# A matmul scheduler that knows the array's shape, scores in larger groups, and a full-height matmul for the count of grid steps

## The chip, the cores and the metric

The kernel runs on one core of a Trainium2 chip. The metric is the time of one execution on the device in microseconds (us). The engines are named as in the profile: PE is TensorE (matmuls; PEld is its weight load), DVE is VectorE, ACT is ScalarE, POOL is GpSimd, SP is SyncE, which issues most transfers.

## The reference, cut to what matters

Three layers follow each other. Attention over 4 batches and 8 heads of 576 positions: half of the heads see the last 32 positions (local), half see every 32nd (strided). Then a gated layer, and a layer of eight experts, to which the tokens are given greedily, the best score first, 288 tokens to each expert.

```python
def reference(q, k, v, w_a, w_b, w_out, w_gate, w1, w2):      # shortened
    scores = q @ k.T / sqrt(64); scores = where(mask, scores, -1e9)
    x = softmax(scores) @ v                    # 2304 tokens x 512
    x = ((x @ w_a) * (x @ w_b)) @ w_out        # 512 -> 1536 -> 512
    logits = (x @ w_gate).flatten()
    for idx in argsort(-logits):               # token, expert; capacity 2304 // 8
        ...                                    # the first free place that fits
    for e in range(8):
        out[assigned == e] = relu(x[assigned == e] @ w1[e]) @ w2[e]
    return out
```

## The kernel before

Every large product is made of three matmuls of a rounded type (f32r): high by high, high by low, low by high part of the operands. So each operand is split into a high part (ACT or POOL) and a low part (DVE) before PE reads it. By the names of PE's results, in order of time:

- `S`: scores of two heads at once, 64 rows by 64 columns of the array for each head, in chunks of 64 positions (local, 96 keys) or 54 (strided). `local_pair` makes nine chunks in groups of three, and `soft` then takes a group chunk by chunk: mask, minimum (DVE), exponential (ACT).
- `PT`, `O`: `P` transposed, and the product with `v` (96 or 54 rows by 64 columns). `out_split` makes `xh` (ACT) and `xl` (DVE) of it, the operands of the next layer.
- `ab`: the gated layer, 48 weight chunks `f`, each with `wh` and `wl`; 24 matmuls of 512 columns or a few more for each. The weights come as 64-bit words; ACT and DVE convert the first twelve chunks (`from_f64`, tiles `r`, `cc`, `w_f`) while PE works on attention and on the first chunks. `tp` and `pw` are the transposes and products of `gate_weights`, `pl` the logits.
- `px`: the second product of the gated layer, 18 times 36 matmuls. Between them stand the steps of `assign`: a search over a grid in seven phases of five steps. A step makes `I` (DVE), counts with 18 small matmuls `pc`, compares (`fe`, DVE), and `pd` carries the count of steps to all 128 rows. In four of five steps `pd` has 64 rows (`step64`, `fe[:T]`), in the last 65 (`step1`).
- `tpi`, `ph`, `po`, `tpo`: the experts. Rows are gathered (`xg`), transposed (`tpi`, one for each of four `kc`), split into `xeh` and `xel`, multiplied (`ph`, result `hh` and `hl`), multiplied again (`po`, copied to `oT`), transposed back (`tpo`, copied to `orow`) and scattered. Weight chunks are split into `w12h` (ACT or POOL) and `w12l` (DVE).

Nothing of this is issued where it is written. `Plan.add` records each operation with a priority (`plan.prio`, a time that `weave` deals out to the bulk of matmuls and to the chains beside it) and with what it depends on. `Plan.flush` then goes through a model of the engines' clocks: at each step it takes the engine that is free first, and of the operations that are ready there the one with the lowest priority number, and calls it. Each engine's queue is in this order on the chip. During the start (`fill`) the plan also puts in dummy matmuls `warm`, so that PE's clock stays up. A matmul's price (`price`) knows its size and type; what stood on PE before it has no influence on it.

Of the kernel before, what the change touches and what calls it, by code (L numbers as in the profile page):

```python
# [8 lines left out]
F32 = mybir.dt.float32  # L9
# [18 lines left out]
T = 64  # L28
STEPS = 5
BIG = 1.0e30  # L30

# [19 lines left out]
class Plan:  # L51
# [12 lines left out]
    def __init__(self, tc):  # L64
        nc = tc.nc
        self.tensor, self.vector, self.scalar, self.gpsimd, self.sync = (
            Engine(self, n, getattr(nc, n)) for n in ("tensor", "vector", "scalar", "gpsimd", "sync"))
        self.prio = 0.0
        self.floor = 0.0
        self.filler = None  # L70
        self.behind = None
        self.ops = []
        self.access = {}
        self.clock = {}
        self.free = {}
        self.live = set()
        self.held = set()
        self.turn = {}
        self.columns = {}
        self.lanes = [0.0] * 8  # L80
# [67 lines left out]
    def add(self, name, engine, method, args, kwargs):  # L148
# [19 lines left out]
        if name == "tensor":  # L168
            wide = method == "matmul" and mybir.dt.size(aps[1].dtype) == 4
            op.load = max(31.0, self.size(aps[1]) * (2 if wide else 1) / 2.4)  # L170
        op.users, op.tiles, op.reads, op.waits, op.ready, op.end = [], {}, set(), 0, self.floor, None
# [55 lines left out]
    def flush(self):  # L227
# [30 lines left out]
        for _ in range(len(self.ops)):  # L258
            while True:
# [18 lines left out]
                while later[e] and later[e][0][0] <= t:  # L278
                    op = heapq.heappop(later[e])[2]
                    heapq.heappush(now[e], (op.prio, op.index, op))  # L280
                op = heapq.heappop(now[e])[2]
                key, t0 = short(op)
                if key is not None:
# [13 lines left out]
            if e == "tensor":  # L297
# [3 lines left out]
                stretch = 1 if warm else 2  # L301
                t = max(t, clock.get("pass", 0.0) + op.load * stretch)
                clock["pass"] = t
                clock[e] = t + op.cost * stretch
# [36 lines left out]
def tile_attention_moe_moe(  # L341
# [192 lines left out]
    def soft(Sp, n, w, masks, P, nm, sm, place):  # L534
        t = apool.tile([128, 288], F32, name="t", bufs=3)[:, :n * w].rearrange("p (c k) -> p c k", c=n)
        for c, i in zip(range(n), place):
# [53 lines left out]
    def local_pair(n0):  # L590
# [4 lines left out]
        sm = apool.tile([128, 11], F32, name="sm", bufs=3)  # L595
        for c0, n in ((0, 3), (3, 3), (6, 3)):
            Sp = ps_acc("S") if b else ps_mm("S")
            for c in range(n):
                for h in range(2):
# [3 lines left out]
                                     start=True, stop=True)  # L603
            if c0 == 6:
                load_next(n0)
# [256 lines left out]
    def later(ns, g):  # L862
        yield 0, ns
        yield from g
# [11 lines left out]
    def begun(r):  # L876
# [8 lines left out]
                 later(8000, attention(0, (3,)))])  # L885
    split_w(0)
    weave(gated(0), [attention(1, (0, 2)), later(4000, attention(1, (1, 3)))], 0, 2000)
    weave(gated(1), [])
# [18 lines left out]
    nc.gpsimd.iota(grid, pattern=[[1, 96], [0, 2]], base=0, channel_multiplier=0, allow_small_or_imprecise_dtypes=True)  # L907
    step64 = acon.tile([T, 128], BF)
    nc.gpsimd.memset(step64, float(T))
    nc.gpsimd.memset(step64[0:1], 0.0)  # L910
    step1 = acon.tile([T + 1, 128], BF)
    nc.gpsimd.memset(step1, 1.0)
    nc.gpsimd.memset(step1[T:T + 1], 1.0 / 16)
    shifts = acon.tile([128, STEPS - 1, NC], I32)
    for s in range(STEPS - 1):
        nc.gpsimd.memset(shifts[:, s], 6 * (STEPS - 2 - s))
    fe = acon.tile([T + 1, 9], BF)
    nc.gpsimd.iota(fe[T:T + 1], pattern=[[1, 9]], base=0, channel_multiplier=0, allow_small_or_imprecise_dtypes=True)
# [57 lines left out]
    def assign():  # L976
# [76 lines left out]
        for ph in range(E - 1):  # L1053
# [3 lines left out]
            for step in range(STEPS):  # L1057
# [20 lines left out]
                if step + 1 < STEPS:  # L1078
                    nc.tensor.matmul(pd[:, 8:9], step64, fe[:T, 8:9], start=True, stop=True)
                    w = spool.tile([128, NC], BF, name="w")  # L1080
# [436 lines left out]
```

## Time and profile before

| | |
|---|---|
| median of 3 runs | 865.04 us (863.64 to 866.58) |
| the profiled execution | 861.87 us, of which the span of the core is 860.2 |
| PE busy | 839.2 us (98%), 6391 matmuls |
| PEld busy | 700.3 us (81%) |
| DVE busy | 501.2 us (58%) |
| ACT busy | 314.4 us (37%) |
| POOL busy | 167.8 us (20%) |
| share of PE in the chain that ended last | 91% |

A product of type f32 (`S`, `O`, `pl`, `pw`) leaves two records in the trace for each matmul of the program. Matmuls overlap in the pipeline: a busy time of 0.39 us for an `ab` says little, since the next one starts 0.23 us after it. Distances from start to start are what PE's timeline is read by. In a timeline, equal instructions that follow each other are one row with a count.

### The profile page before, as it was taken

What the parts mean: (1) busy time and instruction counts of PE and PEld (TensorE: products, weight loads), DVE (VectorE), ACT (ScalarE), POOL (GpSimd) and SP (SyncE); (2) the same over time, 40 slices, a digit from 0 to 9 for tenths busy, and PEclk for the clock granted to TensorE, in tenths of its full rate; (3) what the DMA queues carried; (4) which work ended last, traced back from release to release, by engine and by line L of the source; (5) the groups of instructions that cost most, each with busy time, mean ns of one, the idle gap of its engine ahead of it and who ended that gap; (6) DMA issues with size and microseconds to landing.
All of it is one profiled execution on the core that took longest, in us unless ns stands there. A gap on an engine that the chain in (4) does not pass through costs nothing.

```text
span 860.2 us, 16558 instructions
## 1 busy us (share of the span) xinstructions
PE 839.2 (98%) x6391; PEld 700.3 (81%) x6391; DVE 501.2 (58%) x1450; ACT 314.4 (37%) x840; POOL 167.8 (20%) x220
## 2 busy tenths in 40 slices
PE   8899999999999999999999999999999999999996
PEld 5677888777677777888777777778799999999995
DVE  5999984776464432222377777766166556655540
ACT  6978412465354311111333232222243333333330
POOL 2111321111111120111000000000145435653311
PEclk9999999999999999999999999999989999999998
DMA  9977963656342221121132212100156456655510
GB/s 316 372 278 240 319 222 121 210 176 205 121 154 83 74 74 50 50 74 50 64 121 72 77 50 74 51 24 27 52 188 210 140 179 203 229 173 173 176 30 27
DMA packets 34639, 118.90 MB, mean 138 GB/s; under 512 B 4768, under 2 KB 4768, under 8 KB 34560
## 3 DMA queue, kind: packets, MB, share of 16 engines
q1 hardware_dynamic: 31488, 108.43, 36.7%
q0 software_dynamic: 3072, 9.41, 3.5%
q8 instruction: 50, 0.82, 0.4%
q14 instruction: 29, 0.24, 0.1%
HBM read 98.98 MB, written 18.87 MB: 137 GB/s over the span
## 4 chain that ended last, share of the span: by engine, by line
PE 91%; DVE 3%; DMA 2%; ACT 2%; issue 1%; POOL 0%; POOLq 0%; DVEq 0%; SPq 0%; ACTq 0%
PE ab L158 34%; PE px L158 18%; PE po L158 12%; PE ph L158 12%; PE S L158 3%; PE pc L158 3%; PE pl L158 2%; PE O L158 2%; PE PT L158 2%; DMA r<-in_w_out_dram 1%; PE tpo L158 1%; PE tpi L158 1%; DVE cc L158 1%; PE pw L158 1%; ACT Ps L158 1%
## 5 line engine op out<-in xcount | busy, mean ns | idle before, releaser
L158 PE MATMUL ab<-xh,wh 128*128 128x512 f32 (+1 forms) x488 | 188.0, 386 | 0.6 <-ACT xh L158 0.6
L158 PE MATMUL ab<-xl,wh 128*128 128x512 f32 (+1 forms) x488 | 179.8, 369 | 0.0
L158 PE MATMUL ab<-xh,wl 128*128 128x512 f32 (+1 forms) x488 | 179.1, 367 | 0.0
L158 DVE TENSOR_TENSOR w12l<-w,w12h 128x1024 fp32r<-128x1024 f32 x64 | 78.1, 1222 | 54.3 <-PE po L158 22.3
L158 PEld LDWEIGHTS ab<-xh,wh 128*128 128x128 f32 x488 | 92.2, 189 | 20.0 <-issue 3.1
L158 PEld LDWEIGHTS ab<-xh,wl 128*128 128x128 f32 x488 | 92.3, 189 | 15.3
L158 POOL TENSOR_SCALAR wh<-wab 128x1024 fp32r<-128x1024 f32 x42 | 50.0, 1191 | 274.0 <-PE ab L158 220.4
L158 PEld LDWEIGHTS ab<-xl,wh 128*128 128x128 f32 x488 | 92.5, 190 | 12.5 <-issue 0.4
L158 DVE TENSOR_TENSOR G<-a_sb,ab 128x256 f32<-128x256 f32 x108 | 41.0, 415 | 96.0 <-PE ab L158 89.6
L158 PE MATMUL px<-wol,gh 128*128 128x512 f32 x216 | 87.1, 404 | 0.0
L158 PE MATMUL px<-woh,gh 128*128 128x512 f32 x216 | 86.9, 403 | 0.0
L158 ACT ACTIVATE a_sb<-ab 128x512 f32<-128x512 f32 (+1 forms) x61 | 33.3, 546 | 130.6 <-PE ab L158 116.8
L158 ACT ACTIVATE gh<-G 128x512 fp32r<-128x512 f32 x54 | 34.1, 632 | 124.5 <-PE px L158 119.1
L158 PE MATMUL ph<-xeh,w12h 128*128 128x288 f32 x256 | 78.3, 307 | 0.2 <-ACT xeh L158 0.2
L158 PE MATMUL po<-hh,w12h 128*128 128x288 f32 x256 | 77.7, 304 | 0.0
L158 PE MATMUL ph<-xeh,w12l 128*128 128x288 f32 x256 | 76.4, 299 | 0.0
L158 PE MATMUL ph<-xel,w12h 128*128 128x288 f32 x256 | 76.0, 297 | 0.2 <-DVE xel L158 0.2
L158 PE MATMUL po<-hh,w12l 128*128 128x288 f32 x256 | 75.6, 295 | 0.0
L158 PE MATMUL po<-hl,w12h 128*128 128x288 f32 x256 | 75.4, 295 | 0.0
L158 ACT ACTIVATE w12h<-w 128x1024 fp32r<-128x1024 f32 x36 | 38.1, 1060 | 53.4 <-PE po L158 36.2
L158 DVE TENSOR_TENSOR wl<-wab,wh 128x1024 fp32r<-128x1024 f32 x42 | 51.3, 1222 | 8.0 <-POOL wh L158 7.0
L158 POOL TENSOR_SCALAR w12h<-w 128x1024 fp32r<-128x1024 f32 x28 | 37.5, 1341 | 89.2 <-PE po L158 44.0
(367 smaller groups left out, 1565.7 us busy)
## 6 DMA issues: line engine op xcount, KB each, us to landing
w<-in_w_dram SPq DMA_DIRECT2D x64, 512.0 KB, 3.8
wab<-wab_dram SPq DMA_DIRECT2D x42, 512.0 KB, 3.7
r<-in_w_ab_dram SPq DMA_DIRECT2D x24, 512.0 KB, 7.2
qkT<-in_qk_dram SPq DMA_DIRECT2D x16, 608.0 KB, 5.8
r<-in_w_out_dram SPq DMA_DIRECT2D x12, 512.0 KB, 3.5
wab_dram<-w_f SPq DMA_DIRECT2D x12, 512.0 KB, 4.9
x_dram<-xr SPq DMA_DIRECT2D x17, 256.0 KB, 2.0
wo_dram<-w_f SPq DMA_DIRECT2D x6, 512.0 KB, 4.4
```

Source lines behind the costliest of these rows:

```text
L158: op.call = lambda: getattr(engine, method)(*args, **kwargs)
```

## The change

Three edits.

1. The plan's model of PE gets a shape: method, more than 64 rows, more than 64 columns, and whether the operand is f32r. A matmul of another shape than the one before costs 90 ns more in the model. When the operation that is first by priority has another shape than the last one issued, and a ready one has the last one's shape and a priority number less than 4000 above, that one is taken first.
2. The scores of the local heads come in two groups of five and four chunks instead of three of three; the tile `t` grows for it.
3. `step64`, `step1` and `fe` get 128 rows, the added ones zero, and every `pd` reads all 128.

```diff
+SLACK = 4000.0
+        self.slack = 0.0
+        self.shape = None
...
+            rows, cols = aps[1].ap[0][1], self.size(aps[1])
+            op.shape = method, rows > 64, cols > 64, aps[2].dtype == F32R
...
                 op = heapq.heappop(now[e])[2]
+                if e == "tensor" and self.slack and op.shape != self.shape:
+
+                    same = [x for x in now[e] if x[2].shape == self.shape and x[0] < op.prio + self.slack]
+                    if same:
+                        x = min(same)
+                        now[e].remove(x)
+                        now[e].append((op.prio, op.index, op))
+                        heapq.heapify(now[e])
+                        op = x[2]
...
                 t = max(t, clock.get("pass", 0.0) + op.load * stretch)
+                if op.shape != self.shape:
+                    t += 90.0
+                    self.shape = op.shape
...
-        t = apool.tile([128, 288], F32, name="t", bufs=3)[:, :n * w].rearrange("p (c k) -> p c k", c=n)
+        t = apool.tile([128, 480], F32, name="t", bufs=3)[:, :n * w].rearrange("p (c k) -> p c k", c=n)
...
-        for c0, n in ((0, 3), (3, 3), (6, 3)):
+        for c0, n in ((0, 5), (5, 4)):
...
+    plan.slack = SLACK
...
-    step64 = acon.tile([T, 128], BF)
+    step64 = acon.tile([128, 128], BF)
     nc.gpsimd.memset(step64, float(T))
     nc.gpsimd.memset(step64[0:1], 0.0)
-    step1 = acon.tile([T + 1, 128], BF)
+    nc.gpsimd.memset(step64[T:], 0.0)
+    step1 = acon.tile([128, 128], BF)
     nc.gpsimd.memset(step1, 1.0)
+    nc.gpsimd.memset(step1[T:], 0.0)
...
-    fe = acon.tile([T + 1, 9], BF)
+    fe = acon.tile([128, 9], BF)
+    nc.gpsimd.memset(fe, 0.0)
...
-                    nc.tensor.matmul(pd[:, 8:9], step64, fe[:T, 8:9], start=True, stop=True)
+                    nc.tensor.matmul(pd[:, 8:9], step64, fe[:, 8:9], start=True, stop=True)
```

`plan.slack` is set before the first `flush`, so it holds for every operation.

The order of the queues moves with it. First PE under the gated layer, at the scores of the second batch: `S` of 96 columns is a local head, of 54 a strided one. Before:

```order
L158 MATMUL S<-qkT 64x54 x10
L158 MATMUL ab<-xh,wh 128x512
L158 MATMUL ab<-xl,wh 128x512
L158 MATMUL ab<-xh,wl 128x512
L158 MATMUL S<-qkT 64x96 x6
L158 MATMUL ab<-xh,wh 128x512
L158 MATMUL ab<-xl,wh 128x512
L158 MATMUL ab<-xh,wl 128x512
L158 MATMUL S<-qkT 64x96 x6
```

and after:

```order
L161 MATMUL ab<-xh,wh 128x512
L161 MATMUL ab<-xl,wh 128x512
L161 MATMUL ab<-xh,wl 128x512
L161 MATMUL S<-qkT 64x96 x8
L161 MATMUL S<-qkT 64x54 x10
L161 MATMUL ab<-xh,wh 128x512
L161 MATMUL ab<-xl,wh 128x512
L161 MATMUL ab<-xh,wl 128x512
```

Two groups of scores that came at different places stand together, and fewer places in the row of `ab` are broken.

Then PE at the second `pd` of the assignment. Before:

```order
L158 MATMUL pc<-Cb,I 64x8
L158 MATMUL px<-wol_4747,gh 128x512
L158 MATMUL px<-woh_4746,gl__4768 128x512
L158 LDWEIGHTS step_3770
L158 MATMUL pd<-fe,step_3770 128x1
L158 MATMUL px<-woh_4746,gh 128x512
L158 MATMUL px<-wol_4747,gh 128x512
L158 MATMUL px<-woh_4746,gl__4768 128x512
L158 MATMUL px<-woh_4749,gh 128x512
L158 MATMUL px<-wol_4750,gh 128x512
L158 MATMUL px<-woh_4749,gl__4768 128x512
L158 LDWEIGHTS I
```

and after:

```order
L161 MATMUL pc<-Cb,I 64x8
L161 MATMUL px<-woh_4712,gl__4732 128x512
L161 MATMUL px<-woh_4726,gh 128x512
L161 LDWEIGHTS step_3747
L161 MATMUL pd<-fe,step_3747 128x1
L161 MATMUL px<-wol_4727,gh 128x512
L161 MATMUL px<-woh_4726,gl__4748 128x512
L161 MATMUL px<-woh_4726,gh 128x512
L161 MATMUL px<-wol_4727,gh 128x512
L161 MATMUL px<-woh_4726,gl__4748 128x512
L161 LDWEIGHTS I
```

The step keeps its place; five `px` instead of six stand between `pd` and the next `pc` here, and in later phases seven.

Last DVE at a border between two experts (the third of seven): each `xel` is one `kc` of the next expert's rows, and the last of them is `kc` 3. Before:

```order
L158 TENSOR_TENSOR w12l<-w_7375,w12h 128x1024
L158 TENSOR_TENSOR xel<-tpi,xeh 128x288
L158 TENSOR_TENSOR w12l<-w_7386,w12h 128x1024
L158 TENSOR_TENSOR xel<-tpi,xeh 128x288
L158 TENSOR_TENSOR w12l<-w_7397,w12h 128x1024
L158 TENSOR_TENSOR xel<-tpi,xeh 128x288
L158 TENSOR_TENSOR w12l<-w_7410,w12h 128x1024
L158 TENSOR_TENSOR xel<-tpi,xeh 128x288
L158 TENSOR_TENSOR w12l<-w_7404,w12h 128x1024
L158 TENSOR_TENSOR w12l<-w_7414,w12h 128x1024
```

and after:

```order
L161 TENSOR_TENSOR xel<-tpi,xeh 128x288
L161 TENSOR_TENSOR w12l<-w_7426,w12h 128x1024
L161 TENSOR_TENSOR w12l<-w_7437,w12h 128x1024
L161 TENSOR_TENSOR w12l<-w_7448,w12h 128x1024
L161 TENSOR_TENSOR xel<-tpi,xeh 128x288 x2
L161 TENSOR_TENSOR w12l<-w_7461,w12h 128x1024
L161 TENSOR_TENSOR w12l<-w_7455,w12h 128x1024
L161 TENSOR_TENSOR w12l<-w_7465,w12h 128x1024
L161 COPY orow<-tpo 96x512
L161 TENSOR_TENSOR xel<-tpi,xeh 128x288
```

The `xel` of `kc` 3 moves behind two more splits of weights and behind the copy of a `tpo`; on PE its `tpi` moves behind the first 18 `ph` of the new expert.

## Rows read from the trace of the kernel before

**Rows 1.** PE's timeline at a 64-row pd: start, length, instruction, idle before

```profile
548.90 0.39 PE L158 MATMUL px<-woh,gl__5026 128*128 128x512 f32 x1
549.22 0.17 PE L158 MATMUL pd<-fe,step 64*128 64x1 bf16 x1
549.33 0.50 PE L158 MATMUL px<-woh,gh 128*128 128x512 f32 x1
549.66 0.39 PE L158 MATMUL px<-wol,gh 128*128 128x512 f32 x1
```

**Rows 2.** PE's timeline at a 65-row pd

```profile
537.87 0.40 PE L158 MATMUL px<-woh,gh 128*128 128x512 f32 x1
538.11 0.18 PE L158 MATMUL pd<-fe,step 65*128 65x9 bf16 x1
538.15 0.47 PE L158 MATMUL px<-wol,gh 128*128 128x512 f32 x1
538.46 0.39 PE L158 MATMUL px<-woh,gl__4995 128*128 128x512 f32 x1
```

**Rows 3.** PE's timeline at two S visits among ab

```profile
65.05 0.79 PE L158 MATMUL S<-qkT 64*64 64x54 f32 x20
65.77 0.50 PE L158 MATMUL ab<-xh,wh 128*128 128x512 f32 x1
...
66.34 0.39 PE L158 MATMUL ab<-xh,wl 128*128 128x512 f32 x1
66.66 0.71 PE L158 MATMUL S<-qkT 64*64 64x96 f32 x12
67.30 0.50 PE L158 MATMUL ab<-xh,wh 128*128 128x512 f32 x1
67.64 0.39 PE L158 MATMUL ab<-xl,wh 128*128 128x512 f32 x1
```

**Rows 4.** PE's timeline, two groups of S together (20 and 12 records)

```profile
10.64 1.30 PE L158 MATMUL S<-qkT 64*64 64x54 f32 x32
11.87 0.39 PE L874 MATMUL warm<-ones_f 128*128 128x256 bf16 x2
```

**Rows 5.** PE's timeline at a visit of transposes among po

```profile
681.89 0.41 PE L158 MATMUL tpi<-ident,xg 96*128 96x96 f32 x3
682.08 0.38 PE L158 MATMUL po<-hh,w12h 128*128 128x288 f32 x1
682.30 0.29 PE L158 MATMUL po<-hl,w12h 128*128 128x288 f32 x1
```

**Rows 6.** Busy time in a window: us, PE, PEld, DVE, ACT, POOL, clock, DMA, GB/s

```profile
50.00:100.00 50.00, 50.00 (x427) 37.95 (x428) 48.95 (x149) 35.38 (x113) 9.66 (x13) 1.00 0.79 272
```

**Rows 7.** Timelines of DVE and PE at the twelfth weight chunk

```profile
118.12 1.21 DVE L158 TENSOR_TENSOR wl<-wab,wh 128x1024 fp32r<-128x1024 f32 x1
...
120.39 0.39 PE L158 MATMUL ab<-xh,wl 128*128 128x512 f32 x1
```

**Rows 8.** Timelines of ACT and PE around 217 us

```profile
216.43 0.67 ACT L158 ACTIVATE r<-r 128x512 int32<-128x512 uint32 x1 [2.11 <-DMA r<-in_w_out_dram]
...
217.58 0.61 PE L158 MATMUL pw<-lsel,wT 128*128 128x8 f32 x4 [1.80 <-ACT wT L158]
```

**Rows 9.** Busy time in the window behind it

```profile
220.00:222.00 2.00, 2.00 (x5) 1.61 (x6) 0.73 (x7) 1.19 (x6) 0.00 (x0) 0.50 0.77 203
```

**Rows 10.** Busy time in a window with eight tp in a row

```profile
160.00:163.00 3.00, 3.00 (x34) 2.22 (x33) 2.53 (x5) 1.75 (x4) 1.31 (x1) 1.00 0.51 175
```

**Rows 11.** Timelines of DVE and PE at a border between two experts

```profile
683.67 0.45 DVE L158 TENSOR_TENSOR xel<-tpi,xeh 128x288 fp32r<-128x288 f32 x1
684.04 1.22 DVE L158 TENSOR_TENSOR w12l<-w,w12h 128x1024 fp32r<-128x1024 f32 x1
687.94 0.68 DVE L158 COPY orow<-tpo 96x512 f32<-96x512 f32 x1
...
683.75 0.30 PE L158 MATMUL ph<-xeh,w12h 128*128 128x288 f32 x1
```

More of the change, by code (lines that the diff above doesn't have):

```diff
@@ L603, in local_pair @@
                                      start=True, stop=True)
-            if c0 == 6:
+            if c0 == 5:
                 load_next(n0)
```

## The prediction, made before the changed kernel was run

> **What bounds the kernel now.** I read the page's busy times first: TensorE (PE) is the engine that hardly rests. The windows by stage say the same of the middle: from 50 to 100 us PE is busy for all 50 us, and VectorE (DVE) for 48.95 of them [rows 6]. So until some 115 us there are two engines at their limit, and afterwards one. Up to about 42 us the start-up is paced by DVE and ScalarE (ACT), and PE fills the time with dummy matmuls; what the change does to PE there is worth nothing. From there to the end a nanosecond that PE saves is a nanosecond of the span, unless another engine is late next.
>
> A busy PE is not a PE at its peak, so the second view is PE's timeline, read by the distance from one start to the next. A px matmul starts 0.23 us after the one before it. Around a pd matmul of 64 rows the starts lie 0.32 (px to pd), 0.11 (pd to px) and 0.33 us (px to px) apart [rows 1]; around the last pd of a phase, which has 65 rows, they lie 0.24, 0.04 and 0.31 us apart [rows 2]. The second group is the key to the case. 65 rows already take the full height of the array, the shape of the px around it. So of 0.76 us the change of shape costs 0.17: 0.08 to 0.10 on the way in, 0.065 on the way out, 0.02 on the next weight load. Unrounded starts, averaged over the visits, give 766 against 592 ns: **174 ns for one pd**. The 0.31 us after the full-height pd is a weight load that a short matmul can't hide; it is there in both.
>
> The S visits show the same among the ab matmuls: 66.34 to 66.66 is 0.32 us (0.10 too long), the last S to the ab behind it, and then 0.34 instead of 0.23 us to the second ab (0.11 too long) [rows 3]. What the way out of S costs is seen where two groups of S stand together: 20 records alone hold PE from 65.05 to 65.77, 12 alone from 66.66 to 67.30 [rows 3], together 1.36 us; one after the other they hold it from 10.64 to 11.87, 1.23 us [rows 4]. So one exit is 0.13 to 0.14 us. **An S or O visit costs 0.10 + 0.14 for the two shape changes and 0.11 for the weight load of the ab behind it.**
>
> Transposes have ab's full shape. Three tpi between po matmuls stretch the two starts 681.89 to 682.08 and 682.08 to 682.30 [rows 5]; po alone runs at 0.13, so a visit of three costs some 0.28 us, 0.09 each, and has no price of its own. The new scheduler treats a transpose as another shape and charges 90 ns for it; the chip does not, so gathering transposes earns nothing.
>
> **The change part by part.** *The pd of 128 rows.* 28 of the 35 pd are of the 64-row kind: 28 x 0.174 = **-4.9 us**, with px on both sides in all 28. px here are not waiting for anybody, so all of it counts if DVE keeps pace: in between DVE makes the operand of the next pc, under six px before. In the first phase only five stand there now, 0.17 + 0.23 us less cover for each of some five steps; I take 0.3 us for that into the last term. The extra memsets on GpSimd stand far ahead of the first pd, behind other work, and cost nothing; if they were late, the first pc would wait once.
>
> *The preference for the shape that stands, and S in groups of five and four.* From the order of the two programs I count, between the last dummy matmul and the first logits, 69 visits to another shape before and 48 after, and 50 direct returns from one of them to an ab before, 25 after. 21 x 0.24 = 5.0 and 25 x 0.108 = 2.7: **-7.7 us**. Under the logits there is one visit less and five returns less: **-0.6 us**.
>
> *What DVE takes back.* 15 of the 42 shape changes and 9 of the 25 returns that go lie before 92 us, worth 2.8 us. There DVE converts and splits the weights, and its margin shrinks chunk by chunk: the twelfth wl ends at 119.33 (118.12 + 1.21), and the first ab that reads it starts at 120.39 [rows 7]. PE can come 1.06 us earlier and no more unless DVE does. DVE's work up to that place is the same in both orders. So between 0 (DVE's few idle moments close) and 1.7 us are given back: **+1.5**, near the upper end since DVE idles for 1 us in 50 [rows 6]. Behind that chunk the conversions are done and the margin grows again.
>
> *A stall that loses its place.* At 216 us ACT stands behind the landing of a w_out transfer, the copy of wT behind it, and PE waits 1.80 us for wT [rows 8]; its granted clock then falls to half, 0.50 from 220 to 222 us [rows 9], about 1 us more. Before, 4 ab stand between the two pw groups there; after, 15 (3.4 us). If the transfer lands as late, PE has work: between 0 and -2.8, I take **-2.0**.
>
> *What the reordering adds at the borders of the experts.* Before, the last tpi of the next expert (kc = 3) stands 12 po ahead of the first ph. After, it stands behind 18 ph, followed by four tpo, and ten ph later its xel is read. In DVE's queue that xel now stands behind three w12l and an orow copy. Count from the first ph, 683.75 in the trace of before, where a w12l starts 0.3 us later, at 684.04, because it needs a buffer that the last po frees [rows 11]. PE reaches the reader after 18 x 0.132 + 0.3 (tpi) + 0.43 (tpo) + 10 x 0.132 = 4.4 us. DVE: if one w12l is done by 1.0, two more end at 3.45, orow (0.68) at 4.15, xel (0.45) at 4.6 [rows 11], 4.75 with the hand-over: PE waits 0.35 us. If none is done before 0.3, xel ends at 5.1 and PE waits 0.85; and if a weight chunk lands late, 1.4. If DVE is ahead, 0. Seven borders: between 0 and 9.8, I take **+2.5**, by the buffer that [rows 11] shows.
>
> *Other new waits.* The plan now knows a shape change, so it brings PE to its operands closer to when they are there; before, PE came later than planned by 0.35 us a visit, and that was a cushion. O behind its PT copy, the first steps of the assignment, eight po ahead of the third tpi at the first expert, and S of five chunks at the start (0.3 us later to DVE): between 0 and 4, I take **+1.5**.
>
> Sum: -4.9 - 7.7 - 0.6 + 1.5 - 2.0 + 2.5 + 1.5 = **-9.7 us**. The profiled execution took 861.87 us (span 860.2), which is 0.37% under the median of the runs, 865.04. 852.2 / 861.87 = 0.989, on the median 855.3.
>
> A rule speaks against the grouping of transposes. The Trainium skill, TensorE: Matmul & The Clock Gate, section Part 4: PE-mode transpose, holds that transposes don't count as work for the clock gate. By that rule the longer runs, up to 15 where tpi, tp and PT now meet, would let the clock fall. In this trace a window with eight tp in a row has a granted clock of 1.00 [rows 10]; no run here shows 15.
>
> **The rivals.** *The conversions on DVE hold PE (chance 0.15).* All 2.8 us of the first part are given back, and the start loses its 0.3 us more: about 1.6 worse, 857. For it: DVE's 48.95 of 50 [rows 6]. Against it: the part after 120 us holds two thirds of the gain.
>
> *Slower: the late kc = 3 (0.07; 0.06 for its smaller form).* The place is DVE's queue at the seven borders. To end 0.3% above before, it has to eat 9.7 + 2.6 + 2.5 = 14.8 us, 2.1 a border: that is so from the point where the first of the three w12l starts 1.6 us after the first ph. It needs the weight transfers to be late every time. At 1.4 us a border the whole stands at about 862.6, within 0.3%. Against it: the w12l at 684.04 began without an idle moment of DVE before it [rows 11], so its weights were there.
>
> *Half clock behind long transposes (0.05).* Four runs of 9 to 15 transposes stand under ab; each fall would cost what the one after 216 us did, about 1.7 us: +6.8 in all, 858.9 on the profiled time and 862.1 on the median. It is the mechanism of the rule of the Trainium skill named above; the trace so far speaks against it [rows 10].
>
> *The pd doesn't change (0.05).* If it were the rows that hold data and not the rows addressed that count, the 4.9 us stay: 860.2. Against it: the 65-row pd holds data in 65 rows and goes at the full-height price.
>
> **How the numbers follow.** Forecast 0.62, 855.3 with its own range 851 to 859. The range that is to hold 8 in 10 takes in the bounds: nothing given back and the stall gone is -16, 849 on the median; upward the two rivals at 857 and 860 and half of the one at 862: 849.5 to 862. About 0.3%, 862.4 to 867.6, is what a measurement of this kernel can't tell from no change. Faster: 0.62 + 0.15 + 0.05 + 0.03 = 0.85. Same: 0.08. Slower: 0.07.
>
> **What would show it.** After the change px to pd should be 0.24 us and pd to px 0.04 at all 35 places, and every step of the assignment 0.17 us of PE shorter. S groups of 54 and 96 should stand together with one entry and one exit. At about 120 us the wl should end when PE asks for it, with a wait of up to 1.7 us. The wait of 1.80 us for wT should be gone, and the clock whole around it. At the borders of the experts the even row of ph should show one hole of some 0.35 us ahead of the ph that reads the xel of kc = 3. I am wrong if the pd keep 0.32 and 0.11, if the holes at the borders are 2 us, or if the first ab after the start-up comes more than 1 us later.

## The result, and the profile after the change

The changed kernel takes 854.9 us (median of four runs, 851.71 to 856.31), the kernel before 864.52 (863.64 to 866.58): a ratio of **0.988, 95% interval 0.9843 to 0.9917**. A later group of runs gave 854.55 against 860.66, 0.9915 (0.9886 to 0.9945). The ratios are the recorded ones; they lie up to 0.0017 from the quotients of the medians. The forecast was 855.3. The number fits; the way to it, as the traces show below, was another one in most of its steps.

The page after: the profiled execution took 856.28 us, above its median (before: 861.87, under its median), so the two traces stand only 5.6 us apart.

```profile
span 854.6 us, 16531 instructions
PE 824.9 (97%) x6384; PEld 697.5 (82%) x6384; DVE 501.0 (59%) x1450; ACT 311.3 (36%) x840; POOL 164.3 (19%) x223
```

PE's timeline at a pd that had 64 rows, to be held against [rows 1]:

```profile
548.55 0.39 PE L161 MATMUL px<-wol,gh 128*128 128x512 f32 x1
548.78 0.18 PE L161 MATMUL pd<-fe,step 128*128 128x1 bf16 x1
548.82 0.48 PE L161 MATMUL px<-woh,gl__5017 128*128 128x512 f32 x1
549.13 0.40 PE L161 MATMUL px<-woh,gh 128*128 128x512 f32 x1
```

The starts lie 0.23, 0.04 and 0.31 us apart, where they lay 0.32, 0.11 and 0.33 apart.

The window of [rows 6] (us, PE, PEld, DVE, ACT, POOL, clock): DVE is as busy as before, and PE, 50.00 before, idles for 3 us and loses clock.

```profile
50.00:100.00 50.00, 47.05 (x413) 36.91 (x412) 48.98 (x136) 31.22 (x102) 8.10 (x12) 0.97 0.77 251
```

What PE waits for between 45 and 445 us (engine, what waits, what for: us in total, times, longest), before and after:

```profile
PE pw L158 <- ACT wT L158: 1.8, 1, 1.8
PE pw L158 <- ACT woT L158: 0.6, 1, 0.6
```

```profile
PE O L161 <- ACT PT L161: 2.7, 2, 1.4
PE PT L161 <- DVE Ps L161: 1.1, 1, 1.1
PE pw L161 <- ACT woT L161: 0.9, 1, 0.9
PE S L161 <- PE O L161: 0.9, 1, 0.9
PE pl L161 <- ACT L L161: 0.9, 1, 0.9
PE ab L161 <- DVE wl L161: 0.7, 2, 0.6
PE O L161 <- DVE nm L161: 0.6, 1, 0.6
PE ab L161 <- ACT a_sb L161: 0.5, 1, 0.5
PE px L161 <- ACT gh L161: 0.3, 1, 0.3
```

That is 8.6 us of waits in place of 2.4. In the same window PE waits 2.4 to 3.6 us in the five traces whose attention has no preference (before, pd alone, pd with two splits on ACT, groups alone, no preference up to the logits) and 6.1 to 9.4 us in the nine that have it, so these waits come with the preference.

The wait for wT and the half clock behind it [rows 9] are gone, but the clock falls in two other places. In both, a wait stands ahead of it (1.14 us until 62.54, 0.94 until 194.27). The columns are those of [rows 6], so the clock is the third number from the end:

```profile
61.00:66.00 5.00, 3.86 (x34) 2.79 (x33) 4.58 (x12) 2.99 (x8) 0.00 (x0) 0.66 0.50 182
194.00:199.00 5.00, 4.73 (x33) 3.95 (x34) 2.95 (x22) 4.10 (x24) 1.05 (x1) 0.67 0.79 275
```

The missing 0.34 and 0.33 of five us, at 1.2 in place of 2.4 GHz, are 1.7 us of work lost at each.

**Where the time went, by stage.** Four marks are read in PE's timeline: the starts of the 55th px, of the first tpi and of the 97th ph, and the end. All kernels that ran are in the table, so that the experiments can be read from it too; "old" and "new" say which order PE has at the expert borders.

| kernel | to 55th px | to first tpi | to 97th ph | to the end | span | borders |
|---|---|---|---|---|---|---|
| before | 445.6 | 176.0 | 34.3 | 204.3 | 860.2 | old |
| after | 446.4 | 170.2 | 30.4 | 207.6 | 854.6 | new |
| after, second trace | 443.7 | 170.2 | 30.5 | 208.8 | 853.2 | new |
| pd alone | 445.6 | 171.0 | 34.2 | 204.1 | 854.8 | old |
| pd, two splits on ACT | 450.9 | 171.0 | 31.9 | 204.4 | 858.2 | old |
| preference alone | 444.0 | 174.7 | 31.9 | 208.8 | 859.4 | new |
| groups alone | 440.0 | 176.0 | 31.6 | 205.3 | 853.0 | old |
| no preference up to the logits | 442.6 | 170.2 | 32.0 | 208.4 | 853.1 | new |
| no preference in the experts | 442.8 | 170.2 | 34.0 | 204.3 | 851.1 | old |
| operands 500 ns later | 437.9 | 170.2 | 31.9 | 207.9 | 847.8 | new |
| eight splits on ACT | 441.5 | 170.1 | 30.3 | 208.1 | 850.0 | new |
| reach 1000 ns | 449.9 | 170.3 | 31.0 | 207.6 | 858.7 | new |
| transfers 2 us later | 445.8 | 170.2 | 34.1 | 208.2 | 858.2 | new |
| the best together | 436.7 | 170.2 | 32.4 | 204.4 | 843.6 | old |

In the first column traces of the same order differ by up to 5.3 us (before, pd alone and pd with two splits have one order there; after, its second trace and "no preference in the experts" another; the trace of pd with two splits is of its slowest run, 6.3 us above the median). The second repeats within 0.2 us where nothing in its stage differs, the fourth within 1.3. So the stage before the experts (second column) gave 5.8 us, the first expert (third) 3.9, the borders (fourth) took 3.3 to 4.6, and the attention and the logits (first), where the forecast saw most of the gain, gave nothing in one trace and 1.9 in the other. One trace of each kernel is too few for that stage: the three traces of the order before have a mean of 447.4, the three of the changed order 444.3, 3.1 us less.

### The profile page after: what moved, and what is told of

Its sections match the earlier page's. It is cut to its first block, busy times and chain, and to the rows that moved or that the text cites. A ratio compares the mean times of both kernels' runs of the same rounds, so it can differ in the third digit from the quotient of the medians.

```text
span 854.6 us, 16531 instructions
## 1 busy us (share of the span) xinstructions
PE 824.9 (97%) x6384; PEld 697.5 (82%) x6384; DVE 501.0 (59%) x1450; ACT 311.3 (36%) x840; POOL 164.3 (19%) x223
## 4 chain that ended last, share of the span: by engine, by line
PE 74%; DVE 8%; issue 7%; DMA 6%; POOL 3%; ACT 2%; SPq 0%; POOLq 0%; ACTq 0%; DVEq 0%
PE ab L161 25%; PE px L161 17%; PE po L161 12%; PE ph L161 10%; PE pc L161 3%; DMA r<-in_w_ab_dram 3%; DVE cc L161 2%; DMA r<-in_w_out_dram 2%; DVE wl L161 1%; PE pl L161 1%; PE S L161 1%; PE tpo L161 1%; PE O L161 1%; DVE w_f L161 1%; PE tpi L161 1%
## 5 line engine op out<-in xcount | busy, mean ns | idle before, releaser
L161 PE MATMUL ab<-xh,wh 128*128 128x512 f32 (+1 forms) x488 | 183.8, 377 | 1.5 <-ACT xh L161 0.7
L161 ACT ACTIVATE gh<-G 128x512 fp32r<-128x512 f32 x54 | 34.1, 633 | 115.6 <-PE px L161 104.7
L161 PE MATMUL ph<-xeh,w12h 128*128 128x288 f32 x256 | 75.1, 304 | 1.0 <-issue 0.3
L161 PE MATMUL ph<-xeh,w12l 128*128 128x288 f32 x256 | 74.5, 296 | 0.0
L161 DVE SCALAR_TENSOR_TENSOR hl<-ph,hh 128x288 fp32r<-128x288 f32 x64 | 27.9, 453 | 36.9 <-ACT hh L161 34.7
```

Source lines behind the costliest of these rows:

```text
L161: op.call = lambda: getattr(engine, method)(*args, **kwargs)
```

## The experiments

The times, medians in us, each with the kernel before on the same chip:

| kernel | time | before | ratio, 95% interval |
|---|---|---|---|
| pd alone | 855.65 | 861.47 | 0.994 (0.992 to 0.996) |
| no preference up to the logits | 854.09 | 861.47 | 0.9897 (0.9875 to 0.9918) |
| no preference in the experts | 852.69 | 861.47 | 0.9891 (0.9874 to 0.9907) |
| operands 500 ns later | 850.83 | 861.47 | 0.9873 (0.9856 to 0.9889) |
| after, again | 854.55 | 860.66 | 0.9915 (0.9886 to 0.9945) |
| pd, two splits on ACT | 853.61 | 860.66 | 0.9918 (0.9888 to 0.9948) |
| eight splits on ACT | 851.68 | 860.66 | 0.9891 (0.9844 to 0.9937) |
| preference alone | 861.24 | 860.66 | 1.000 (0.998 to 1.002) |
| groups alone | 857.58 | 863.64 | 0.9937 (0.9905 to 0.9968) |
| reach 1000 ns | 861.01 | 863.64 | 0.9973 (0.995 to 0.9996) |
| transfers 2 us later | 854.61 | 863.64 | 0.989 (0.986 to 0.9919) |
| the best together | 845.68 | 863.64 | 0.9793 (0.9764 to 0.9823) |

**The three edits, one by one.** My theory after the two traces was that the preference's gain in the attention comes back as waits; the rival was the recorded sum. The third edit, on the kernel before:

```diff
-                    nc.tensor.matmul(pd[:, 8:9], step64, fe[:T, 8:9], start=True, stop=True)
+                    nc.tensor.matmul(pd[:, 8:9], step64, fe[:, 8:9], start=True, stop=True)
```

> The kernel before with the third edit alone: the step matrices and fe have 128 rows, the order of the work stays as it was. My sum: 28 pd at 0.174 us, so -4.9 us, some 859.6 against 864.5, all of it gained between the first pc and the first tpi (px to pd 0.24 us, pd to px 0.04). Rival, the chain: the pd chain is paced by VectorE, so PE only meets its operands earlier, waits for them, and no more than 1 us of the 4.9 is left at the first tpi. The half clock after the first tpi (620 to 632 us before) should stay, since the order there is untouched: if it goes with this edit alone, the gain is nearer to 8.

Measured: 0.994, some 5.2 us; 176.01 to 170.99 us between the 55th px and the first tpi. All 5.02 us are there at the first tpi, so the rival (DVE's chain paces the pd) is out.

The first edit alone, the scheduler's lines with SLACK = 4000:

> The kernel before with the first edit alone: preference for the standing shape and the charge of 90 ns; S in groups of three, pd of 64 rows. 49 visits up to the logits in place of 69. By the recorded sum: -7.7 of visits, -0.6, -2.0 for the stall, +2.5 at the borders and +3 of other waits, so -4 to -5. By the account after the traces, in which the attention's gain is handed back whole, the first expert gains 2 to 4 and the borders cost 3.5: 0 +/- 1.5 against the kernel before. That tells what is left of the change without pd: if it is 0, pd carries half of the 10 us and the rest comes from the S groups or from both together.

Measured: 1.000, nothing. By stages of its trace: -1.6 before the 55th px, -1.3 up to the first tpi, -2.4 at the first expert, +4.5 at the borders. PE waits 6.8 us between 45 and 445 us, and not once for wT. The account after the traces holds, the recorded sum (-4 to -5) doesn't.

The second edit alone:

```diff
-        for c0, n in ((0, 3), (3, 3), (6, 3)):
+        for c0, n in ((0, 5), (5, 4)):
```

> The kernel before with the second edit alone: local S in groups of five and four chunks, order by the old rules, pd of 64 rows. 67 visits to another shape up to the logits in place of 69, so by the price of a visit -0.5 to -0.7 us on PE; the start-up has 222 PE operations in place of 286, fewer of them dummies. If S groups are worth only their visits, the time is that of the kernel before within 1 us. If the rest of the change's gain (the whole 7 to 10, pd 5, the preference alone 0) is in them, it is 2 to 4 us faster, and that must show in the trace by the first ab or by the 96th.

Measured: 0.9937, 5.4 us (2.8 to 8.2), far more than two visits. Its trace is of the fastest of its six runs, 2.9 us under their median, and 2.7 us of what it is shorter lie at the first expert, where the order is the old one. Two other places are the edit's. The 97th ab starts at 66.75 us (69.64 before), since real ab take the place of dummy matmuls sooner (the last dummy starts at 33.2, before at 42.0). And the stall of [rows 8] is halved, with the clock whole around it:

```profile
213.63 0.61 PE L158 MATMUL pw<-lsel,wT 128*128 128x8 f32 x4 [0.85 <-ACT wT L158]
```

```profile
211.00:217.00 6.00, 5.15 (x48) 3.51 (x45) 3.72 (x14) 3.05 (x10) 0.00 (x0) 1.00 0.47 170
```

That is 0.95 us of wait and 1.7 of clock less than in the trace of before. The clock is not shown to be the groups' doing: pd alone has the order before there, and its clock stayed whole behind a wait of 1.48:

```profile
219.50 0.61 PE L158 MATMUL pw<-lsel,wT 128*128 128x8 f32 x4 [1.48 <-ACT wT L158]
```

```profile
217.00:225.00 8.00, 6.52 (x47) 4.62 (x48) 4.68 (x17) 3.46 (x12) 1.05 (x1) 1.00 0.52 177
```

The sooner start and the shorter wait are the groups' doing. The kernel without preference up to the logits (below) has the order of groups alone up to there, and its trace has the 97th ab at 68.12 us and a wait for wT of 0.91; the three traces of the order before have 69.64, 69.69 and 72.64 us, and 1.80, 1.48 and 1.75. So the start gives 1.5 to 5.9 us. With the preference on top that ab is later again: at 70.50, 69.65 and 68.54 us in the three traces of the changed order.

The three parts give 5.2, 0 and 5.4 us, together 10.6; the whole change gave 7.3 and 10.4 by its two ratios. Within the intervals they add up, and the preference's share is nothing.

**The preference, stage by stage.** Off up to the first logits:

```diff
     split_w(0)
-    plan.slack = SLACK
+    plan.price_shape = 0.0
...
     apool_cm.__exit__(None, None, None)
+    plan.slack, plan.price_shape = SLACK, 90.0
```

> The changed kernel, but up to the first logits the scheduler has no preference and no charge of 90 ns; logits, assignment and experts keep both, S keeps groups of five and four, pd keeps 128 rows. Between start-up and logits it has 67 visits to another shape, the changed kernel 48, the kernel before 69. The recorded sum gave these visits 7 us: by it this kernel is 6 to 8 us slower than the changed one, 861 to 863. My theory after the two traces: the PE time that the grouping saves is handed back there as waits of PE for operands that are not ready yet and two falls of its clock, so this kernel stands within 2 us of the changed one, 853 to 857, and PE has some 6 us less idle time and more work between 50 and 440 us.

Measured: 0.9897, within 2 us of the changed kernel in either group of runs, though it has 67 visits and that one 48. PE waits 0.3 to 1.0 us in six places of the attention and logits, 3.6 us in all, where the changed kernel waits 8.6 and 6.7. The grouping does save PE work, and it is handed back.

Off in the experts (and the same up to there):

```diff
+    plan.slack = plan.price_shape = 0.0
     bpool_cm.__exit__(None, None, None)
     spool_cm.__exit__(None, None, None)
```

> The changed kernel, but without preference and charge from the first expert on, so that transposes and po there alternate as in the kernel before; all before the first expert is unchanged. Two effects. The seven borders: the changed kernel loses 0.3 to 0.9 us at each against the kernel before, 3 us in all, which should come back: -3. The first expert: before, its half clock at 620 to 632 us cost some 3.4 us, and in the changed kernel, with eight po in a row behind the third tpi, there is none. If the order makes the difference, half clock comes back, +3.5 to +4.5, and the sum is +0.5 to +1.5 (855.5 to 856.5). If the clock's fall in the kernel before had another cause (what stood ahead of the wait, the landing of xg), it stays whole, and the sum is -3 (852).

Measured: 204.3 us from the 97th ph on, as before, so the seven borders' 3.3 us (4.6 in the second trace) come from the preference alone; and 34.0 us at the first expert, with the clock at half again (0.57 from 618 to 624 us). Both halves came as expected for the case that the order counts; the time, 0.9891, can't be told from the changed kernel's. For the clock, though, the order is not the cause: it fell there with the preference on in two kernels (no preference up to the logits, transfers 2 us later) and stayed whole without it in pd alone and groups alone.

What a border costs is seen in the changed kernel's trace (DVE, then PE). In these rows a new ph group needs a buffer that hl frees, and hl stands in DVE's queue behind a w12l:

```profile
683.59 1.22 DVE L161 TENSOR_TENSOR w12l<-w,w12h 128x1024 fp32r<-128x1024 f32 x1 [0.96 <-POOL w12h L161]
684.73 0.45 DVE L161 SCALAR_TENSOR_TENSOR hl<-ph,hh 128x288 fp32r<-128x288 f32 x1
...
684.80 0.29 PE L161 MATMUL ph<-xeh,w12l 128*128 128x288 f32 x1
685.23 0.40 PE L161 MATMUL ph<-xeh,w12h 128*128 128x288 f32 x1
```

There are 0.43 us between two starts in place of 0.13, at four of the borders, and 0.61 at a fifth (1.73 in the second trace, most of the way from 3.3 to 4.6). Ahead of the ph that reads the late xel there are 0.24 in place of 0.13. The rest is the grouping itself. A tpi behind a tpi holds PE for 0.083 us and a tpo for 0.109, but the last transpose ahead of a ph or po only for 0.03: the bulk matmul starts under it. Every group that is joined with another loses such an end, 0.05 to 0.08 us; three a border make 0.2.

**The first expert.** Before, and with pd alone, one xel operation on DVE (called a copy below and in the expectations; it subtracts xeh from oT) is long there. DVE, GpSimd and PE with pd alone:

```profile
623.62 2.83 DVE L158 TENSOR_TENSOR xel<-oT,xeh 128x288 fp32r<-128x288 f32 x1 [0.51 <-ACT xeh L158]
...
624.07 2.08 POOL L158 TENSOR_SCALAR w12h<-w 128x1024 fp32r<-128x1024 f32 x2
...
626.51 0.40 PE L158 MATMUL ph<-xel,w12h 128*128 128x288 f32 x1 [2.08 <-DVE xel L158]
```

```diff
-            split_chunk(e, i, raw_q.pop(0), "act" if i % 2 else "pool", "dve")
+            split_chunk(e, i, raw_q.pop(0), "act" if i % 2 or (e, i) in ((1, 0), (1, 2)) else "pool", "dve")
```

> The kernel before with pd of 128 rows, and in addition the first two splits of expert 1's weights by ScalarE in place of GpSimd. PE's order is that of the kernel with pd of 128 rows alone. There, at the first expert, an xel copy of VectorE takes 2.83 us where its like takes 0.46, while GpSimd runs two weight splits (2.08 us), and PE waits 2.08 us for it. Theory, collision: with GpSimd's splits gone from there the copy takes 0.46, PE's wait of 2.08 goes, and the first ph of the next group comes 2 us earlier against the first tpi: 2 us faster than pd of 128 rows alone, so some 7.2 below the kernel before. Rival: the copy is long because of the transfers or its own operands; it stays 2.8 us and the time that of pd alone (5.2 below). A third way: PE's clock, whole there in that trace, falls to half behind the waits of tpi as in the kernel before, and takes the place of the wait: no gain, with the copy short.

Measured: PE's order is the same, the copy takes 0.46, the wait is gone, 34.2 us become 31.9. The time is 0.9918 against 0.994, which the intervals don't part.

```profile
628.98 0.46 DVE L158 TENSOR_TENSOR xel<-oT,xeh 128x288 fp32r<-128x288 f32 x1 [0.51 <-ACT xeh L158]
```

So the collision is shown, at its place. In the kernel before, the copy was as long (2.82) while PE ran at half clock, and PE's wait at the end of it was 0.23 only:

```profile
628.73 2.82 DVE L158 TENSOR_TENSOR xel<-oT,xeh 128x288 fp32r<-128x288 f32 x1 [0.51 <-ACT xeh L158]
...
631.61 0.42 PE L158 MATMUL ph<-xel,w12h 128*128 128x288 f32 x1 [0.23 <-DVE xel L158]
```

```profile
625.00:631.00 6.00, 5.81 (x25) 5.29 (x23) 4.97 (x8) 3.34 (x7) 4.66 (x5) 0.50 0.35 100
```

Either cost alone is some 2 to 3 us, and they lay over each other. In the changed kernel the six tpi stand together, the copies are done at 622.9, and GpSimd's split (625.32) runs into a w12l that nobody waits for. Without the preference in the experts the copy was short, and half clock cost the same again; in the kernel with transfers planned later the copy was long (2.91) in spite of the preference. With neither cost the old order takes 31.6 and 31.9 us (groups alone, pd with two splits), and the changed kernel takes 30.4 and 30.5: so at most 1.5 of the 3.9 us are the order's, and the rest hangs on whether the collision and the clock's fall happen to come.

**What makes the waits of the attention.** Four theories, one kernel each. All operands 500 ns later in the plan, up to the logits:

```diff
-        return self.HOPS.get((a.engine, b.engine), 160.0) + (b.load if b.engine == "tensor" else 0.0)
+        return self.HOPS.get((a.engine, b.engine), 160.0) + (b.load + self.late if b.engine == "tensor" else 0.0)
```

> The changed kernel with one number more in its plan: up to the first logits, an operand that another engine makes counts as ready for PE 500 ns later than planned so far. 44 visits instead of 48. Theory of the lost cushion: the changed plan brings PE to its operands with nothing to spare, and seven new waits of 0.5 to 1.5 us between 45 and 245 us come from that; with 500 ns of room each is shorter by about 0.5 (3.5 us in all), and the two falls of the clock behind them (1.7 us each) may go: 848 to 852. Rival, the other engines are at their limit there: VectorE works 97 to 98% of the time up to 120 us, so PE waits for it in another place, and the time stays within 1.5 us of the changed kernel. A third way, lost work: holding operands back makes PE take other work that is wanted later, and the start-up is longer: slower by 1 to 2 us.

Measured: 0.9873, the lowest time of one edit, though not clear of the changed kernel's first ratio, 0.988, and not for the reason given. The waits are there, 7.2 us in all: 0.98 for S (0.94 before this edit), 0.97 for pl (0.87), 0.88 for O (1.45). What its trace gains is mostly at the start: the first ab comes at 23.2 us (27.8), the 97th at 65.2 (70.5), and there is no half clock before 100 us. The lost cushion is not shown; why the start is shorter stays open.

A shorter reach of the preference, SLACK = 1000:

> The changed kernel with a reach of 1000 ns in place of 4000 for the preference: an operation of the standing shape is taken before its turn only if its turn is less than 1 us away. 56 visits up to the logits in place of 48, 61 returns to ab in place of 38, so by the prices of visits 8 x 0.24 + 23 x 0.11 = 4.4 us more PE work. Theory, postponed chains: the waits of 0.5 to 1.5 us in the attention come from operations that the preference puts off by up to 4 us; with a reach of 1 us they go, 3 to 5 us, and the time stays as it is or is up to 1 us better. Rival: the waits come from what stands ahead of the operands in the queues of ScalarE and VectorE, conversions above all, whatever the reach; then the waits stay and the 4.4 us of visits come on top.

Measured: 0.9973, by the ratios 5 to 8 us slower than the changed kernel, and the waits stay, 9.4 us in all (1.9 for woT, 1.6 for Ps, 1.4 for nm and others). This is the rival's case: visits come on top, and waits are set by something else.

What that is, ACT shows in the changed kernel ahead of its longest wait (ACT, then PE):

```profile
238.85 0.68 ACT L161 ACTIVATE r<-r 128x512 int32<-128x512 uint32 x1 [4.01 <-DVE wl L161]
239.44 0.25 ACT L161 ACTIVATE PT<-PT 96x128 f32<-96x128 f32 x1
...
237.91 0.38 PE L161 MATMUL tp<-ident,w_f 128*128 128x128 f32 x2
239.74 0.34 PE L161 MATMUL O<-PT,vt 96*64 96x64 f32 x4 [1.45 <-ACT PT L161]
```

ACT idles 4 us in front of a conversion r (here until DVE's wl is done), and the copy of PT stands behind it in its queue: the pattern of [rows 8]. At 82 us it is the same with a landing. So transfers were planned 2 us later:

```diff
         if a.dma:
-            return 1050.0
+            return 1050.0 + self.land
```

> The changed kernel with one number of its plan changed: up to the logits a transfer counts as landed 2 us later than planned so far. 49 visits, as before. In the trace of the changed kernel ScalarE stands 0.8 to 6.1 us in front of the landing of raw weights (r), and copies of PT that PE waits for stand behind it: 1.25 us at 82 us, 1.45 at 240. Theory, queue order: with the landing planned later the conversions take their turn behind those copies, both waits go, with them some 2 to 3 us; ScalarE's waits for r shrink from 21 us to under 8. Rival: conversions that come later hold up VectorE, which is the limit until 120 us, and the gain is lost there: no change, or slower by up to 2 us, with PE waiting for wl at about 100 to 120 us.

Measured: 0.989, no change. ACT's waits for r do shrink, from 21 to 8 us, and the wait of 1.45 goes. But that of 1.25 becomes one of 1.74 for P from DVE, the conversions come later on DVE too, and PE waits there:

```profile
123.54 0.50 PE L162 MATMUL ab<-xh,wl 128*128 128x512 f32 x1 [1.65 <-DVE wl L162]
```

The rival fits: until 120 us DVE is at its limit, and what ACT gets back DVE loses. (The trace is of the slowest of the five runs, 5.3 us above the median; both costs of the first expert fall in it.)

DVE also loses time to GpSimd there. From 40 us up to the 289th ab, eight conversions and splits of the changed kernel that ran into a split of GpSimd's take 5.3 us longer than their like; in the trace of before five operations lose 2.7. That the change makes this worse is not shown: pd alone and pd with two splits, with the order before, lose 5.0, and groups alone loses 4.6 though its 289th ab is there at 117.56 us (before 119.93, changed kernel 124.33). Eight of GpSimd's splits to ACT:

```diff
-            split(wh, wl, r)
+            split(wh, wl, r, "act" if 6 <= i < 14 else "pool")
```

> The changed kernel with eight weight splits (chunks 6 to 13, which fall between some 80 and 125 us) by ScalarE in place of GpSimd. In the trace of the changed kernel VectorE loses 5.3 us up to the 288th ab to operations with both operands in SBUF that run into a GpSimd split (eight of them, up to 1.53 us where 0.69 is usual); in the kernel before five of them cost 2.5. VectorE is busy 98% there. Theory, collisions: 2 to 3 us of that go, the 288th ab comes 2 to 3 us earlier than in the changed kernel, and the end 1 to 3 us. Rival, ScalarE: it works 80% of the time there with its own chain of P and PT copies, and one more us for each split makes those late: O and PT wait longer, no gain or 1 us slower. Second rival: VectorE's work before 120 us doesn't hold PE at all: both places stay as they are.

Measured: 1.8 us lost in place of 5.3, and the 289th ab at 122.28, which is 1.0 to 2.0 earlier than in the three traces of that order (124.33, 123.89, 123.29). The time is 0.9891 against 0.9915 in the same group of runs, 2 us, which the intervals don't part. That DVE gets its time back is shown; that PE gains by it is likely, and its worth at the end is open.

The changed kernel once more on that chip, for its second trace:

> The changed kernel once more, beside the others of this group on the same chip, and for a second trace of it. From the ratio measured so far, 0.988, it should be 10 us below the kernel before. Theory one, fixed waits: the trace shows the same gaps of PE (1.1 at some 62 us, 1.2 at 80, 0.9 at 192, 1.4 at 238, 0.9 at 432) within 0.3 us, and the same loss at the expert borders. Theory two, chance: the gaps come from where transfers and VectorE's collisions with GpSimd happen to fall, and half of them move or go.

Measured: 0.9915. The waits stand where they stood: 0.80 for Ps (1.14), 0.90 for P and 0.46 for PT ahead of the O that had waited 1.25, 0.88 for S (0.94), 1.44 for O (1.45), 0.87 for pl (0.87). They come from the order. The two falls of the clock are chance: there is none in those places, and one between 30 and 50 us.

**What the runs favoured, together:** operands 500 ns later, the ten splits on ACT, the preference up to the first expert only.

> What the runs so far favoured, put together: the changed kernel with operands planned 500 ns later up to the logits, eight weight splits between 80 and 125 us and the first two of expert 1 by ScalarE, and no preference and no charge from the first expert on. If the parts add: the ratio of the kernel with later operands alone, 0.987, less 3.5 us for the borders, less 2 for the splits before 125 us; at the first expert the preference's 2.4 go and the short xel copy brings them back. So 5 us under it, a ratio of 0.981, some 845 where the kernel before takes 861. If they take the place of one another (ScalarE late through ten splits more, or a new order with new waits), it is not under 849.

Measured: 845.68 against 863.64, **0.9793 (0.9764 to 0.9823)**, faster than both kernels, and as the parts add (0.981 expected): 204.4 us at the borders, 32.4 at the first expert, 436.7 up to the 55th px. The third edit and the groups without any preference weren't run together.

## Why the prediction was right, and where it wasn't

- *pd of 128 rows, -4.9:* it was -5.02, right in price, count and place. [Rows 2], where 65 rows went at the full-height price, was the row that told it.
- *Visits -7.7 and logits -0.6; waits +1.5 and +1.5:* the price of a visit was near as PE work: PE is busy 421.0 us of the first 440 and was 429.1 (1.7 of the 8.1 are dummy matmuls, and 8.3 were forecast). The step that failed is "a nanosecond that PE saves is a nanosecond of the span, unless another engine is late next". The term for that, +1.5 (0 to 4), is mis-sized: 8.6 us of waits are there (6.7 in the second trace) where 0.6 and the stall were, and in the first trace one half clock more; the preference alone measured 1.000. 5.4 of the 8.6 us are for PT, Ps, L and wl, and PT, Ps and L stood behind conversions and weight splits in the queues of ACT and DVE: PE comes sooner and waits. What ended the other 3.2 us was not followed up. Rows 6 and 7 had been read for one chain (wl) only, and not for what else stands in those queues.
- *The start-up is worth nothing:* this was wrong. S in groups of five and four lets ab take the place of dummy matmuls sooner there. I gave the second edit 0.3 us of loss; alone it gains 5.4, of which 0.6 to 0.95 is the shorter wait at the stall.
- *The stall, -2.0:* it is gone, as forecast, and by the preference: the preference alone has no wait for wT either, and the groups alone leave 0.85. Its price was uncertain: before, it cost 1.80 and 1.7 for the clock (I had put the clock at 1), in pd alone 1.48 and nothing.
- *Borders, +2.5:* they took 3.3 and 4.6. The place and size were near, the mechanism half right: the xel of kc = 3 ends 4.4 us after the first ph (679.63 + 0.44 less 675.67), where I had 4.6, and the hole there is 0.10 in place of 0.35; a ph buffer freed late costs 0.3 more, and joined transposes 0.2, which I had costed at nothing.
- *Not forecast:* the first expert, -3.9, where a collision of DVE with GpSimd and a half clock, which lay over each other before, both stayed away, mostly by chance; and the preference's 0.8 between px and tpi.
- *Rivals:* transposes don't lower the clock here. The run of 15 that the rival spoke of is there, and its window has a clock of 1.00, in the second trace too:

```profile
184.32 0.64 PE L161 MATMUL PT<-ident,P 128*96 128x128 f32 x4
184.80 0.60 PE L161 MATMUL tp<-ident,w_f 128*128 128x128 f32 x4
185.26 0.53 PE L161 MATMUL PT<-ident,P 128*96 128x128 f32 x3
185.63 0.60 PE L161 MATMUL tp<-ident,w_f 128*128 128x128 f32 x4
```

```profile
184.00:187.00 3.00, 3.00 (x42) 2.56 (x39) 2.97 (x8) 2.28 (x7) 0.00 (x0) 1.00 0.54 141
```

The clock fell behind waits, and not behind all of them: 1.25 us at 82 and 1.45 at 240 left it whole. The conversions on DVE, the rival of 0.15, do hold PE, but waits for wl are 0.7 of the 8.6 us.

In sum: forecast -4.9 (pd), -7.3 (attention, logits, stall, waits), +2.5 (borders); measured in the trace -5.0, +0.8, +3.3, and -3.9 and -0.8 that weren't in it. That is -5.6, the distance of the two traces. The medians lie 9.6 apart, the second group 6.1; executions differ by that much, above all before the 55th px. By the means of three traces that stage gives -3.1 in place of +0.8, and the sum is -9.5. One part, the pd, was right for its reason. For the rest, gains that were not forecast (the start, the first expert) stand where the forecast had the preference's; that the number came out right is luck.

## What to carry to other kernels

Price a saving on the busiest engine only up to the next operand: go through the in-order queues of the engines that feed it and ask, for each operand, what stands ahead of it there. Where a scheduler is changed, test its rules stage by stage; here the rule with most code gained nothing (1.000, 0.998 to 1.002), since what it saved in one stage it lost in another, and the two small edits beside it, with 5.2 and 5.4 us alone, carried the whole. A small matmul of half height that stands alone among full-height ones is worth padding with zero rows: here 0.18 us each, 28 times.

## What the runs showed of the hardware

A DVE operation with both operands in SBUF that meets a GpSimd weight split can stand until the split is over: 1.53 us in place of 0.69 for a conversion, and 2.83 in place of 0.46 for the long xel (two splits in a row). G, hl and the xel made from tpi, which read one operand from PSUM, keep their 0.42, 0.46 and 0.46 us beside a split.

It goes the other way too. In the changed kernel's trace all 20 conversions, splits and products of this kind that began ahead of the split they met kept their time, and the split can take longer instead. This one took 4.72 us in place of 1.05 while DVE went from one operation to the next (GpSimd):

```profile
106.99 4.72 POOL L161 TENSOR_SCALAR wh<-wab 128x1024 fp32r<-128x1024 f32 x1 [4.69 <-DMA wab<-wab_dram]
```

The Trainium skill, SBUF — State Buffer, section "Who interferes with whom", states this lock between the two engines, and that whoever issues first keeps it. Both halves agree with those 20; the long xel does not fit the second half, since it began 0.45 us ahead of the split (623.62 and 624.07, by a profile whose spans on GpSimd are rough) and still lost. Two other traces have the same (2.82 and 2.91 us).
